# Moving the third exp reading from GpSimd to VectorE in a fused attention and FFN kernel

## The chip, the cores and the metric

The kernel runs on one core of a Trainium2 chip. The metric is the device time of one execution in microseconds (us), as the median of several runs. A core has five engines that run side by side and meet by semaphores: TensorE (PE; its weight loads are listed as PEld), VectorE (DVE), ScalarE (ACT), GpSimd (POOL) and SyncE (SP, which issues the DMAs). Matmul results lie in PSUM, eight banks of 128 x 512 f32; everything else lies in SBUF.

## The reference

```python
x = A_x                                  # (1, 2048, 640) bf16
xn = layernorm(x)
# A: 32 query heads of width 20, one shared key and value head
q = (xn @ wq) as (32 heads, 2048, 20);  k = xn @ wk;  v = xn @ wv      # k, v: (2048, 20)
p = softmax(q k^T * 20**-0.5)            # per head 2048 x 2048
a = (p @ v, heads side by side) @ wo
# B: FFN
b = silu(xn @ w1) @ w2                   # 640 -> 1728 -> 640
out = x + a + b
```

## The kernel before

**Tiling.** The 2048 queries are cut into 4 chunks of 512, so a head and a chunk make a unit, 128 units in all. Units go in groups of three (43 groups, the last with two). A group runs over 16 key tiles of 128 keys: 688 steps. In a step TensorE makes up to three score blocks (128 keys x 512 queries, L769), one per PSUM bank, in banks 0 to 2 and 3 to 5 in turn; the exp of each block is taken; and the exps are multiplied with the values (L857) into four 32-row strips of bank 6, where a group's sums pile up. Bank 7 serves all other matmuls: the projections, the FFN (L1084 for its first half, L1146 for its second) and the output projection (L1151).

**Exps by two engines.** ScalarE takes the exp of two or three blocks with one instruction (L787: 1024 or 1536 elements per partition). If `want_dve` says so, the step's third block goes to VectorE instead. There the scores come scaled so that an integer holds the bits of a bf16 number: one instruction (`p1`, L801) clamps a block and turns it into 16-bit integers Z, which read as bf16 are a coarse exp. To make it finer, the same bits are read three times: Z itself, Z + 43 and Z + 86, each with its own weighting of the values, and the three products are summed by TensorE. Z and the first addition's result (Y, index 0) enter at the step's own accumulation; the third reading (Y, index 1) enters as a "third" (`th` in `flush_z`), hosted by a step that has room for one more matmul, or by a separate accumulation `PT` for up to three of them.

**Who makes the readings.** Z + 43 is made by VectorE for up to three blocks at once (`flush_z`, L869, up to 1536 elements), when `ZB` blocks have gathered, after `ZWAIT` steps, or at a group's end. Z + 86 is made by GpSimd for each block at once, as `yp` (L807): it adds 86 * 65537 to pairs of 16-bit numbers read as one 32-bit integer. The constant lies in the tile `c86`, filled in the prologue.

**The order.** A planner in Python (`Sched`) builds the order of each engine before the kernel is emitted: it simulates the engines with estimated durations (`t_dve_4x`, `t_act` and so on) and picks for each engine the ready operation of lowest priority number; on VectorE p1 has 1.0, the evacuations of projections and the FFN 0.8, a group's evacuation of bank 6 (L972) 1.1, the readings 4.0. For TensorE `step` picks between score matmuls (first whenever their banks are free), accumulations and other jobs; accumulations are preferred when more than `NBLK - PV_PRESS` of the 31 blocks of the exp ring are in use. An operation with `lock` set is planned not to start while a locked one of the other engine (VectorE, GpSimd) runs: the readings and GpSimd's normalisations (L939 to L958) have it, `yp` has not (`Y_LOCK`). `Y_SLOW` adds 0.1 us to each planned reading. The chip runs each engine's list in the planned order, with waits on semaphores in place of the planned times.

What decides how many blocks VectorE gets:

```python
def want_dve(self, t):
    if t < DVE_FROM or t % KT >= KT - NOD or t >= self.T - DVE_LAST:
        return False
    sc = self.sc
    back = sc.t["dve"] - sc.t["pe"]
    for op in sc.pend["dve"]:
        back += op.dur
    back += len(self.zblocks) * 0.6
    return back < DVE_TH
```

Of the kernel before, what the change touches and what calls it, by code (L numbers as in the profile page):

```python
# [10 lines left out]
I32 = mybir.dt.int32  # L11
AF = mybir.ActivationFunctionType
ALU = mybir.AluOpType

P = 128
# [6 lines left out]
QW = 512  # L22
# [19 lines left out]
PH = ((0, 1.0), (43, 0.8046875), (86, 0.625))  # L42
# [3 lines left out]
NBLK = 31  # L46
NZ = 4
ZB = 3
Y_POOL = True
Y_TIME = 0.72  # L50
Y_LOCK = False
Y_SLOW = 0.1
H_FIRST = 4
NEARLY = 2
LASTPV = 16
# [1 line left out]
ZWAIT = 6  # L57
SWITCH = 0.105
S_LEAD = 0.56
PV_PRESS = 12  # L60
DVE_TH = 2.8
U_PRIO = 1.1
X_PRIO = 0.8
PACE = (0.9, 0.9, 0.9, 0.9)
# [251 lines left out]
def t_dve_4x(n):  # L316
    return n / 3840.0 + 0.065
# [37 lines left out]
class Builder:  # L355
# [13 lines left out]
    def sb(self, shape, dt):  # L369
        self.nsb += 1  # L370
        return self.stack.enter_context(self.nc.sbuf_tensor(f"sbt{self.nsb}", shape, dt))

    def alloc(self):
        sb = self.sb
        self.ps = self.stack.enter_context(self.nc.psum_tensor("psall", [P, 8 * BANK], F32))
        self.xnT = sb([P, DC, S], BF16)
        self.w1 = sb([P, DC, F], BF16)
        self.w2 = sb([P, FC, D], BF16)
        self.wq = sb([P, DC, D], BF16)
        self.qd = sb([P, 2, QW], BF16)  # L380
        self.wo = sb([P, DC, D], BF16)
        self.kT = sb([P, 2, S], BF16)
        self.v = sb([P, 5, KT, SLOT], BF16)
        self.qT = sb([P, HT, 2, QW], BF16)
        self.E = sb([P, NBLK * QW], BF16)
        self.Z = sb([P, NZ, ZB * QW], I16)
        self.Y = sb([P, NZ, 2, ZB * QW], I16)
        self.U = sb([P, 2, QW], BF16)
        self.kv_st = self.U[:, 1, 0:2 * DC * DH].rearrange("p (a c d) -> p a c d", a=2, c=DC)
        self.stk = sb([P, 64], BF16)  # L390
        self.UT = sb([P, 2, 4, P], BF16)
        self.W = sb([P, 4, 3, DH + 1], F32)
        self.hT = sb([P, FC, QW], BF16)
        self.o = sb([P, 4, D], BF16)
        self.oT = sb([P, DC, QW], BF16)
        self.wqp = self.oT[:, :, :].rearrange("p c e -> p (c e)")[:, 0:DC * 2 * P].rearrange("p (c e) -> p c e", c=DC)
        self.tb = sb([P, 2, QW], BF16)
        self.xres = sb([P, 4, D], BF16)
        self.yx = self.w1[:, :, :].rearrange("p a b -> p (a b)")[:, 0:8 * D].bitcast(F32).rearrange(
            "p (i e) -> p i e", i=4)  # L400
        self.ost = sb([P, 3, D], BF16)
        self.wk = self.ost[:, 2, :].rearrange("p (c e) -> p c e", c=DC)
        self.idf = self.w2[:, 4, 0:2 * P].bitcast(F32)
        self.idb = sb([P, P], BF16)
        self.st6 = sb([P, NT, 2, 6], F32)
        self.mv = sb([P, NT, 2], F32)
        self.rstd = sb([P, NT], F32)
        self.nb = sb([P, NT], F32)
        self.ex2 = sb([P, NT], F32)
        self.junk = self.E[:, (NBLK - 2) * QW:(NBLK - 2) * QW + D]  # L410
        self.tmp = sb([P, 4, NT], F32)
        self.rL = sb([P, 2, 4, 3], F32)
        self.offq = sb([P, 1], F32)
        self.offk = sb([P, 1], F32)
        self.eps = sb([P, 1], F32)
        self.c86 = sb([P, 1], I32)
        self.zero = sb([P, 512], BF16)
        self.XS = 11
        hflat = self.hT[:, :, :].rearrange("p a b -> p (a b)")
        oflat = self.o[:, :, :].rearrange("p b c -> p (b c)")  # L420
        self.okeys = [("o", h) for h in range(H)]

        def xslot(n):
            if n < self.XS:
                return hflat[:, n * D:(n + 1) * D]
            if n < NT - 1:
                return self.xres[:, n - self.XS, :]
            return oflat[:, 3 * D:4 * D]

        def xkeys(n):  # L430
            if n < self.XS:
                return [("hT_x", n)]
            if n < NT - 1:
                return [("xres", n - self.XS, 0), ("xres", n - self.XS, 1)]
            return [("x15",)] + self.okeys
        self.xslot = xslot
        self.xkeys = xkeys
# [312 lines left out]
    def do_S(self, t, now):  # L750
        sc = self.sc
        g, kt = divmod(t, KT)
# [40 lines left out]
        if dv:  # L793
            self.dve_steps += 1
            self.group_dve[g] += 1
            self.last_dve_kt[g] = kt
            zs, zp = self.zset, len(self.zblocks)
            bb = par3 + nh - 1

            def p1(v):  # L800
                return v.tensor_scalar(self.Z[:, zs, zp * QW:(zp + 1) * QW], self.bk(bb), 0.0, ZMAX,  # L801
                                       ALU.max, ALU.min)
            sc.new("dve", t_dve_ps(QW), p1, [("B", bb)], [("Z", zs, zp)], prio=1.0, name=f"p1_{t}")
            self.y_on_pool = Y_POOL
            if self.y_on_pool:
                c86 = bass.AP(self.c86, self.c86[:, :].offset, [list(self.c86[:, :].ap[0]), [0, QW // 2]])
                sc.new("pool", Y_TIME, lambda v: v.tensor_tensor(  # L807
                    self.Y[:, zs, 1, zp * QW:(zp + 1) * QW].bitcast(I32),
                    self.Z[:, zs, zp * QW:(zp + 1) * QW].bitcast(I32), c86, ALU.add),
                    [("Z", zs, zp), ("c86",)], [("Y", zs, 1, zp)], prio=4.0, name="yp").lock = Y_LOCK  # L810
        first = kt == 0
        last = kt == KT - 1

# [46 lines left out]
    def flush_z(self):  # L860
        sc = self.sc
        zs = self.zset
        n = len(self.zblocks)
        self.zset = (self.zset + 1) % NZ
        zk = [("Z", zs, i) for i in range(n)]
        Z = self.Z[:, zs, 0:n * QW]
        w = n * QW
        for k in range(1 if self.y_on_pool else 2):
            sc.new("dve", Y_SLOW + t_dve_4x(w), lambda v, k=k: v.tensor_scalar(  # L869
                self.Y[:, zs, k, 0:n * QW], Z, float(PH[k + 1][0]), None, ALU.add), zk,  # L870
                [("Y", zs, k, i) for i in range(n)], prio=4.0 + 0.1 * k, name=f"y{k}").lock = True
        ts = []
        for i, (t, pv) in enumerate(self.zblocks):
            ks = [("Z", zs, i), ("Y", zs, 0, i)]
            pv.deps |= sc.deps_of(ks, ())
            for k in ks:
                sc.readers[k].append(pv)
            x = self.Y[:, zs, 1, i * QW:(i + 1) * QW].bitcast(BF16)
            kt = t % KT

            def th(pe, q, x=x, kt=kt):
                if q >= 2:
                    return self.pv_mm(pe, q, 2, kt, x, False, False)
                self.pv_mm(pe, 0, 3, kt, x, False, False)
                return self.pv_mm(pe, 1, 4, kt, x, False, False)
            ts.append((th, ("Y", zs, 1, i), kt))
        first = self.zblocks[0][1]
        end = self.pv_wait[-1][0].kt == KT - 1
        tail = self.pv_wait.pop() if end else None
        seen = False  # L890
        for op, _ in self.pv_wait:
            seen = seen or op is first
            if seen and self.can_host(op) and ts:
                self.host(op, ts.pop())
        if end and self.can_host(tail[0]) and len(self.thirds + ts) % 3 == 1:
            self.host(tail[0], ts.pop() if ts else self.thirds.pop())
        self.thirds += ts
        while len(self.thirds) >= 3 or (end and self.thirds):
            part = self.thirds[:3]
            self.thirds = self.thirds[3:]  # L900

            def fn(pe, part=part):
                ins = None
                for q, x in zip((2, 3, 0), part):
                    ins = x[0](pe, q)
                return ins
            op = sc.new("pe", 0.3, fn, [x[1] for x in part], [], name="PT", mode="PV", queue=False)
            op.mm = len(part) + len(part) // 3
            op.kt = max(x[2] for x in part)
            op.na = 0  # L910
            op.after = None
            self.pv_wait.append((op, False))
        if tail is not None:
            self.pv_wait.append(tail)
        self.zblocks = []
# [368 lines left out]
    def prologue(self):  # L1284
# [49 lines left out]
        def pool(d, fn, r, w, prio=0.0):  # L1334
            return np_("pool", d, fn, r, w, prio=prio, name="pool")
# [4 lines left out]
        pool(0.2, lambda g: g.tensor_copy(self.idb[:, :], self.idf[:, :]), [("idf",)], [("idb",)])  # L1340
        pool(0.3, lambda g: g.memset(self.zero[:, :], 0.0), [], [("zero",)])
        pool(0.1, lambda g: g.memset(self.eps[:, :], EPS), [], [("eps",)])
        pool(0.1, lambda g: g.memset(self.c86[:, :], PH[2][0] * 65537), [], [("c86",)])
        pool(0.7, lambda g: g.memset(self.wk[:, :, :], 0.0), [], [("wk",), ("ost", 2, 0), ("ost", 2, 1)])
        wqd = self.wqp[:, :, :].rearrange("p c (h j) -> p c h j", j=SLOT)
        wqs = self.wq[:, :, 0:160].rearrange("p c (h d) -> p c h d", d=DH)
# [302 lines left out]
```

## Time and profile before

| | |
|---|---|
| median of 3 runs | 739.14 us (739.08 to 740.04) |
| profiled execution | 740.04 us, its span 738.2 us |
| granted TensorE clock | 0.995 |
| PE busy | 707.6 us, 96% |
| DVE busy | 665.5 us, 90% |
| ACT busy | 691.0 us, 94% |
| POOL busy | 538.4 us, 73% |
| `p1` L801 | 646 instructions |
| first addition L869 | 230 instructions |
| `yp` L807 | 646 instructions |

A row of a group reads: line, engine, operation, tiles out<-in, shapes out<-in, count | busy us of the group, mean ns of one | idle us of the engine just before them, and what ended most of that. A row of a stretch reads: window, its length, then for each engine busy us and instructions, then the granted clock, the DMA share and GB/s. A row of the waits reads: engine, tile and line that waited, what it waited for, total us, times, longest. A row of the timeline reads: start, us until the last of the merged instructions ends, engine and line, operation, count. A busy time holds the tail of an instruction that the next one may already overlap.

### The profile page before, as it was taken

To read this page: it belongs to the slowest core of one execution; us is meant where nothing else is said; L and a number is where in the kernel's file an instruction comes from. 1 tells how busy PE (TensorE), PEld (TensorE's weight loads), DVE (VectorE), ACT (ScalarE), POOL (GpSimd) and SP (SyncE) were. 2 spreads that over 40 slices of the span, in tenths; PEclk is the share of its full clock that TensorE was granted. 3 is DMA by queue.
4 is the path that set the end of the run, shared out by engine and by line. 5 is a ranking of instruction groups with operands and counts; after the bars stand their busy time and mean duration, and the time that the engine had idled before them with its cause. 6 is when DMAs were issued, how large, how long until landed. Compare 5 with 4: busy or idle time off the path is not lost.

```text
span 738.2 us, 18883 instructions
## 1 busy us (share of the span) xinstructions
PE 707.6 (96%) x6798; PEld 229.7 (31%) x6852; DVE 665.5 (90%) x1206; ACT 691.0 (94%) x780; POOL 538.4 (73%) x929
## 2 busy tenths in 40 slices
PE   9788999999999999999999999999999999999998
PEld 4422222233333223223333222222233332322235
DVE  7786998999999999989999999999999999989973
ACT  6886999999999999999999999999999999999940
POOL 5467777787787877777878877787788877777750
PEclk9999999999999999999999999999999999999999
DMA  6494010000003021100001101110002000200101
GB/s 191 80 338 108 20 25 17 21 17 16 9 16 44 17 58 40 32 10 9 9 8 27 33 16 40 54 32 16 8 9 44 10 8 16 80 9 8 31 16 36
DMA packets 58466, 29.14 MB, mean 39 GB/s; under 512 B 44390, under 2 KB 57734, under 8 KB 58374
## 3 DMA queue, kind: packets, MB, share of 16 engines
q1 hardware_dynamic: 56918, 27.71, 14.7%
q8 instruction: 56, 0.92, 0.5%
q10 hardware_dynamic: 1456, 0.22, 0.2%
q14 instruction: 36, 0.29, 0.1%
HBM read 11.36 MB, written 2.62 MB: 19 GB/s over the span
## 4 chain that ended last, share of the span: by engine, by line
PE 62%; ACT 17%; DVE 6%; issue 5%; POOL 1%; DMA 1%; DVEq 0%; ACTq 0%; POOLq 0%
PE psall L857 21%; PE psall L769 20%; ACT sbt L787 15%; PE psall L1146 9%; PE psall L1084 6%; DVE sbt L801 3%; PE psall L1151 2%; PE psall L1050 2%; ACT sbt L1092 1%; DVE sbt L869 1%; DMA sbt<-sbt 1%; DVE sbt L972 1%; PE psall L693 1%; POOL sbt L807 0%; DVE sbt L1057 0%
## 5 line engine op out<-in xcount | busy, mean ns | idle before, releaser
L787 ACT ACTIVATE sbt<-psall 128x1024 bf16<-128x1024 f32 (+2 forms) x688 | 657.8, 1091 | 16.8 <-PE psall L769 15.9
L807 POOL TENSOR_TENSOR sbt<-sbt 128x256 int32<-128x256 int32 x646 | 447.2, 698 | 149.3 <-DVE sbt L801 122.7
L801 DVE TENSOR_SCALAR sbt<-psall 128x512 int16<-128x512 f32 x646 | 432.5, 683 | 34.4 <-PE psall L769 26.4
L769 PE MATMUL psall<-sbt 32*128 32x512 bf16 x2048 | 269.1, 385 | 9.7 <-ACT sbt L787 4.7
L857 PE MATMUL psall<-sbt 128*32 128x512 bf16 x3524 | 270.2, 385 | 4.2 <-DVE sbt L869 2.0
L769 PEld LDWEIGHTS psall<-sbt 32*128 32x128 bf16 x2048 | 68.7, 91 | 252.8 <-issue 105.1
L869 DVE TENSOR_SCALAR sbt<-sbt 128x1536 int16<-128x1536 int16 (+2 forms) x230 | 134.8, 587 | 2.8
L857 PEld LDWEIGHTS psall<-sbt 128*32 128x32 bf16 x3524 | 67.8, 94 | 115.0 <-issue 75.4
L1146 PE MATMUL psall<-sbt 128*128 128x320 bf16 x448 | 86.2, 302 | 0.0
L1084 PE MATMUL psall<-sbt 128*128 128x512 bf16 (+1 forms) x242 | 75.7, 385 | 5.1 <-issue 3.7
L1146 PEld LDWEIGHTS psall<-sbt 128*128 128x128 bf16 x448 | 35.1, 97 | 43.4 <-issue 33.8
L1097 DVE SCALAR_TENSOR_TENSOR sbt<-sbt,psall 128x512 bf16<-128x512 bf16 (+1 forms) x56 | 38.1, 680 | 4.2 <-ACT sbt L1092 3.5
L1092 ACT ACTIVATE sbt<-psall 128x512 bf16<-128x512 f32 (+1 forms) x56 | 37.7, 674 | 0.0
L1084 PEld LDWEIGHTS psall<-sbt 128*128 128x128 bf16 (+1 forms) x280 | 18.8, 98 | 39.9 <-issue 29.6
L972 DVE CAST sbt<-psall 128x512 bf16<-128x512 f32 x43 | 29.3, 681 | 2.0 <-PE psall L857 1.9
L1151 PE MATMUL psall<-sbt 128*128 128x320 bf16 x144 | 28.7, 303 | 0.4 <-DVE sbt L1181 0.4
L1050 PE MATMUL psall<-sbt 128*128 128x512 bf16 (+1 forms) x81 | 26.6, 385 | 2.4 <-issue 1.4
L958 POOL TENSOR_TENSOR sbt<-sbt 128x240 bf16<-128x240 f32 (+2 forms) x44 | 25.7, 583 | 0.9 <-DMA sbt<-sbt 0.5
L944 POOL TENSOR_TENSOR sbt<-sbt 128x44 f32<-128x44 f32 x84 | 25.0, 298 | 1.0
L706 PE MATMUL psall<-sbt 128*128 128x512 bf16 (+2 forms) x67 | 17.5, 407 | 4.8 <-DVE sbt L1565 3.3
L942 POOL CAST sbt<-sbt 128x168 f32<-128x168 bf16 x42 | 14.2, 337 | 9.7 <-DMA sbt<-sbt 9.1
L1178 ACT ACTIVATE sbt<-psall 128x320 bf16<-128x320 f32 x4 | 1.5, 437 | 20.7 <-PE psall L1151 20.7
(94 smaller groups left out, 219.8 us busy)
## 6 DMA issues: line engine op xcount, KB each, us to landing
sbt<-in_A_x_dram SPq DMA_DIRECT2D x32, 160.0 KB, 3.6
out_dram<-sbt SPq DMA_DIRECT2D x15, 160.0 KB, 1.9
sbt<-in_B_w_dram SPq DMA_DIRECT2D x5, 432.0 KB, 7.4
sbt<-sbt SPq DMA_DIRECT2D x105, 20.0 KB
sbt<-in_B_w_dram SPq DMA_DIRECT2D x13, 160.0 KB, 5.8
sbt<-sbt SPq DMA_TRANSPOSE x68, 2.4
sbt<-sbt SPq DMA_DIRECT2D x1, 1024.0 KB, 7.3
sbt<-in_A_wo_dram SPq DMA_DIRECT2D x5, 160.0 KB, 6.8
```

The lines of the kernel that those rows point to most:

```text
L769: ins = pe.matmul(self.bk(par3 + j), self.kT[r:r + SLOT, kk, kt * P:(kt + 1) * P], self.qT[r:r + SLOT, h // 4, (x // H) % 2, :], start=Tru ...
L787: return a.activation(self.E[:, b0 * QW:(b0 + na) * QW], self.ps[:, par3 * BANK:(par3 + na) * BANK], AF.Exp, scale=ACT_SCALE)
L801: return v.tensor_scalar(self.Z[:, zs, zp * QW:(zp + 1) * QW], self.bk(bb), 0.0, ZMAX, ALU.max, ALU.min)
L807: sc.new("pool", Y_TIME, lambda v: v.tensor_tensor(self.Y[:, zs, 1, zp * QW:(zp + 1) * QW].bitcast(I32), self.Z[:, zs, zp * QW:(zp + 1) * ...
L857: return pe.matmul(self.bk(UBANK, 0, QW, q * SLOT, (q + 1) * SLOT), self.v[:, w, kt, :], x, start=start, stop=stop, tile_position=(0, q * ...
L869: sc.new("dve", Y_SLOW + t_dve_4x(w), lambda v, k=k: v.tensor_scalar(self.Y[:, zs, k, 0:n * QW], Z, float(PH[k + 1][0]), None, ALU.add), z ...
L1050: return pe.matmul(self.bk(b, 0, QW, 0, rows), self.wq[:, k, lo:hi], self.xnT[:, k, c * QW:(c + 1) * QW], start=(k == 0), stop=(k == DC - 1))
L1084: return pe.matmul(self.bk(b, 0, QW, 0, rows), self.w1[:, k, fk * P:fk * P + rows], self.xnT[:, k, c * QW:(c + 1) * QW], start=(k == 0), s ...
L1092: sc.new("act", t_act(QW), lambda a: a.activation(t, src, AF.Tanh, scale=0.5), [("B", b)], [("tb", tp)], prio=X_PRIO, name=f"th{c}_{fk}")
L1097: sc.new("dve", t_dve_ps(QW), lambda v: v.scalar_tensor_tensor(out=self.hT[0:rows, fk, :], in0=t, scalar=1.0, in1=src, op0=ALU.add, op1=AL ...
L1146: return pe.matmul(self.bk(b, 0, 320), self.hT[0:rows, fk, i * P:(i + 1) * P], self.w2[0:rows, fk, e0:e0 + 320], start=(m == 0), stop=(m = ...
L1151: return pe.matmul(self.bk(b, 0, 320), self.oT[:, k, i * P:(i + 1) * P], self.wo[:, k, e0:e0 + 320], start=(m == 0 and src != "ps"), stop= ...
```

## The change

`yp` and its constant `c86` are taken out. `flush_z` makes both additions on VectorE, Z + 43 and Z + 86, as two instructions one behind the other over the same gathered blocks. The planner's extra 0.1 us on a reading goes, `PV_PRESS` becomes 8 and `DVE_TH` 3.2. TensorE's use of the readings is the same.

```diff
-Y_POOL = True
-Y_TIME = 0.72
-Y_LOCK = False
-Y_SLOW = 0.1
...
-PV_PRESS = 12
-DVE_TH = 2.8
+PV_PRESS = 8
+DVE_TH = 3.2
...
-        self.c86 = sb([P, 1], I32)
...
             sc.new("dve", t_dve_ps(QW), p1, [("B", bb)], [("Z", zs, zp)], prio=1.0, name=f"p1_{t}")
-            self.y_on_pool = Y_POOL
-            if self.y_on_pool:
-                c86 = bass.AP(self.c86, self.c86[:, :].offset, [list(self.c86[:, :].ap[0]), [0, QW // 2]])
-                sc.new("pool", Y_TIME, lambda v: v.tensor_tensor(
-                    self.Y[:, zs, 1, zp * QW:(zp + 1) * QW].bitcast(I32),
-                    self.Z[:, zs, zp * QW:(zp + 1) * QW].bitcast(I32), c86, ALU.add),
-                    [("Z", zs, zp), ("c86",)], [("Y", zs, 1, zp)], prio=4.0, name="yp").lock = Y_LOCK
...
-        for k in range(1 if self.y_on_pool else 2):
-            sc.new("dve", Y_SLOW + t_dve_4x(w), lambda v, k=k: v.tensor_scalar(
+        for k in range(2):
+            sc.new("dve", t_dve_4x(w), lambda v, k=k: v.tensor_scalar(
                 self.Y[:, zs, k, 0:n * QW], Z, float(PH[k + 1][0]), None, ALU.add), zk,
                 [("Y", zs, k, i) for i in range(n)], prio=4.0 + 0.1 * k, name=f"y{k}").lock = True
...
-        pool(0.1, lambda g: g.memset(self.c86[:, :], PH[2][0] * 65537), [], [("c86",)])
```

## The prediction

> **What bounds the kernel now.** I read the table of busy time by stretch first, because the kernel has a ramp, a long uniform middle and a tail.
>
> ```profile
> core 0: us, PE busy (x) PEld busy (x) DVE busy (x) ACT busy (x) POOL busy (x), PEclk, DMA share, GB/s
> ...
> 60.00:100.00 40.00, 35.96 (x323) 10.32 (x327) 31.77 (x56) 34.45 (x40) 30.72 (x53) 0.96 0.10 20
> 100.00:150.00 50.00, 47.99 (x458) 13.92 (x462) 46.00 (x78) 50.00 (x58) 36.20 (x61) 1.00 0.08 20
> ...
> 300.00:350.00 50.00, 47.60 (x451) 14.63 (x449) 45.81 (x77) 50.00 (x59) 37.96 (x63) 1.00 0.04 10
> ...
> 450.00:500.00 50.00, 48.73 (x472) 14.34 (x475) 48.42 (x84) 50.00 (x56) 38.41 (x64) 1.00 0.17 41
> ```
>
> From 100 to 700 us ScalarE (ACT) is idle for at most 0.3 us in any 50: it sets the pace. TensorE looks almost as busy, but matmul ends are modelled. VectorE (DVE) is close behind, and GpSimd (POOL) has 9 to 14 us free in 50. DMA is idle. Next, the groups by shape say what these engines do:
>
> ```profile
> L787 ACT ACTIVATE sbt<-psall 128x1024 bf16<-128x1024 f32 x632 | 597.4, 1077 | 10.9 <-PE psall L769 10.4
> L807 POOL TENSOR_TENSOR sbt<-sbt 128x256 int32<-128x256 int32 x646 | 447.2, 698 | 149.3 <-DVE sbt L801 122.7 <-PE psall L769 9.8 <-PE psall L857 2.5
> L801 DVE TENSOR_SCALAR sbt<-psall 128x512 int16<-128x512 f32 x646 | 432.5, 683 | 34.4 <-PE psall L769 26.4 <-POOL sbt L944 1.0 <-POOL sbt L939 0.4
> ...
> L869 DVE TENSOR_SCALAR sbt<-sbt 128x1536 int16<-128x1536 int16 x198 | 119.1, 602 | 2.7
> ...
> L787 ACT ACTIVATE sbt<-psall 128x1536 bf16<-128x1536 f32 x41 | 60.8, 1489 | 2.6 <-PE psall L769 2.5
> ```
>
> There are 688 steps of up to three score blocks. A step whose third block goes to VectorE costs ScalarE a 1024-wide exp, otherwise a 1536-wide one: 1.489 - 1.077 = 0.412 us more. So **each block that VectorE gives back costs the bound engine 0.41 us**. VectorE has 646 blocks already; 41 steps are 1536 wide.
>
> The timeline says what an instruction takes from its engine, since its mean duration holds a tail that the next one overlaps:
>
> ```profile
> 301.11 1.27 DVE L801 TENSOR_SCALAR sbt<-psall 128x512 int16<-128x512 f32 x2
> 302.42 0.56 DVE L869 TENSOR_SCALAR sbt<-sbt 128x1536 int16<-128x1536 int16 x1
> 302.90 1.28 DVE L801 TENSOR_SCALAR sbt<-psall 128x512 int16<-128x512 f32 x2
> ```
>
> Two blocks end 1.27 us after the first starts, so the second starts 1.27 - 0.68 = 0.59 later: 0.60 us each (its median from start to start). The 1536-wide reading takes 302.90 - 302.42 = 0.48 (median 0.476).
>
> **The change part by part.** *What moves.* For each VectorE block GpSimd made the third reading (Y, index 1) at L807. These 646 instructions go; `flush_z` makes it as a second instruction behind the first, for up to three blocks at once. The bits are the same, so TensorE's work per block stays.
>
> *VectorE's load now*, in the 600 us from 100 to 700, by starts in the trace: 578 blocks x 0.60 = 347. Of the 204 readings (182 of 1536 elements, 12 of 1024, 10 of 512) the wide ones lie beside GpSimd and last 0.602 on average, against 0.555 for those that don't start inside a GpSimd instruction: 0.475 + 0.047 = 0.52 each, all 204 together 103. FFN products 50 x 0.60 = 30, accumulator evacuations 38 x 0.60 = 23, queries 16 x 0.60 = 10, output sums 49 x 0.40 = 20, reciprocals 38 x 0.14 = 5. Sum 538, 90% of 600. (The busy row's 94% holds the tails.)
>
> *VectorE's load after, if no block moves*: the readings become clean pairs, 182 x 0.95 + 12 x 0.68 + 10 x 0.4 = 185 in place of 103. Sum 620: 103% of the time there is. It can't fit, so the planner, which offers VectorE a block only while its backlog is under `DVE_TH`, hands blocks to ScalarE, whose work is the time.
>
> *How many.* With x blocks given back, each frees 0.60 + 2 x 0.475/3 = 0.92 us of VectorE and lengthens the stage by 0.41: 620 - 0.92x = u(600 + 0.41x), u being the share of VectorE that the planner can fill. At u = 1, x = 15 and the stage is 6.2 us longer. At 0.98, which is what ScalarE fills as the bound (578 x 0.904 + 31 x 1.331 + 50 x 0.477 + 0.75 = 589 of 600), x = 24, 10 us. At 0.90, today's fill, x = 62, 25.4 us. I take 0.96, x = 33.5, **13.7 us**: nearer to ScalarE's row, because a queue that always has a ready reading in it has fewer gaps than today's. Its fullest stretch (450 to 500) is already 97% by the busy row, but its instructions come in bursts behind the FFN jobs, so not 0.98.
>
> *What y pairs do to score banks.* A block behind a reading waits; a block releases the score bank that the matmul two steps on needs. Now:
>
> ```profile
> PEld psall L769 <- ACT sbt L787: 63.9, 166, 0.7
> ...
> PEld psall L769 <- DVE sbt L801: 42.7, 108, 0.6
> ...
> PEld psall L769 <- DVE sbt L869: 9.2, 23, 0.5
> ...
> PEld psall L857 <- POOL sbt L807: 5.8, 21, 1.3
> ```
>
> Readings were the last thing 23 times. A pair keeps a block 0.475 longer: 23 x 0.4 = 9 us more if all of it reached ScalarE; zero if its exp in hand (0.9 us) covers it. I take **1.5**, nearer to zero, because today's 52 us of waits for VectorE leave ScalarE only 16.8 us idle in all. Queued behind such a block on VectorE are the FFN products (L1097), which hold bank 7, and the evacuation of the accumulator (L972).
>
> *The ramp* (40 to 100 us): 51 blocks, 17 readings, 17 x 0.43 = 7 us more in some 11 idle us of VectorE. 0 to 3, I take **0.5**: a block may be given back. *The tail*: the last third reading came 0.61 us after its block from an idle GpSimd, now 0.475 after its first reading, so 0.3 later; 0 to 1, I take **0.2**.
>
> *Priced at nothing.* GpSimd's freed 447 us: only 5.8 + 0.8 us of matmul waits and 4.0 us of reciprocal waits hung on it, and what waited for it waits for the second reading next; a gain of up to 6 stays in the range. TensorE's 34 fewer third readings free some 22 quartets of matmuls, 22 x 0.23 = 5 us, beside a ScalarE that is never idle. The `c86` memset lies in the ramp, where GpSimd is 60% busy. `PV_PRESS` 8 for 12 lets more exp blocks wait before the accumulation is preferred, so TensorE's order changes: -2 to +2, taken as 0, since score matmuls go first in either. `DVE_TH` and `Y_SLOW` act through u.
>
> *Sum*: 13.7 + 1.5 + 0.5 + 0.2 = 15.9. The profiled execution took 740.04 (span 738.2 and 1.8 around it), 0.9 over the median of three runs, 739.14. So 755.9 against the profiled one and **755** as a median.
>
> **A rule against the row.** In the trace 100 of the 198 wide readings start inside a GpSimd instruction; they last 0.643, the others 0.555. A GpSimd addition that starts inside a reading lasts 0.887, an undisturbed one 0.612. So the offload costs VectorE 9 us in all, and saves it some 90.
>
> The Trainium skill (Perfetto Trace Analysis, Optimizing Scalar/DVE Operations) warns that VectorE and GpSimd share an SBUF port, so that moving work between them may not help. Taken at its word, undoing the move would cost nothing and the time would stay at 739. By the rows it is GpSimd that pays most of the sharing, and the sum stays at 755.
>
> **The rivals.** *Faster*: the second readings fit, no block is given back, and TensorE's waits for GpSimd (5.8 us) go: about 733. It needs VectorE at 0.98 of 600 (588) with 538 - 103 + 93 = 528 (the first readings clean) plus the second ones, so at most 60 us for 204, 0.29 each. The row says 0.475, and the second instruction has nothing to overlap but the tail already taken off. Only if a pair ran much closer than a reading and a block do. *Nearly free*: VectorE fills to 0.98 or more, nothing else: 739 + 6.2 to 739 + 10, 745 to 750. For it: with both readings on one engine no lock breaks the queue. *Stalls*: pairs hold up blocks and thereby score matmuls, so VectorE stays at 0.90 and ScalarE gets gaps: 25.4 + 5 = 30, 764 to 773. For it: 31 of these 610 steps are already 1536 wide although VectorE is 90% full, so bursts count. *No effect*: GpSimd's readings held something that I don't see, worth the same 16: 739.
>
> **How the numbers follow.** The forecast (u of 0.98 with a gap of 1 us, 739 + 10 + 1, to u of 0.93, where x = 47.6 costs 19.5, with gaps of 5: 750 to 764) gets 0.60, nearly free 0.19, stalls 0.13, faster 0.05, no effect 0.03. A measurement can tell a change of about 0.2% (1.5 us) from none. Slower: 0.60 + 0.19 + 0.13 = 0.92; same 0.03; faster 0.05. The range from 745 to 766 takes in the forecast and nearly free, leaving out most of the stalls and both cases at or under 739.
>
> **What would show it.** Right: no int32 group on GpSimd, whose busy time falls to about 90; some 430 readings in the reading group, with a mean of 0.55 to 0.57; about 610 blocks at L801's successor instead of 646 and about 77 exps of 1536 elements instead of 41; ScalarE still without idle time from 100 to 700 and about 14 us busier; VectorE's busy row at 97% or more. Wrong: as many blocks as before; ScalarE idle for over 10 us in the middle (then stalls on score banks are the price, not blocks); or VectorE under 94%.

## The result and the profile after

The kernel after takes 745.80 us (median of four runs, 744.75 to 746.59) against 739.59 for the kernel before in the same comparison: ratio 1.0079, 95% interval 1.0056 to 1.0103. It is slower by 6.2 us, where the prediction had 15.9. The profiled execution took 745.05 us with a span of 743.2, 5.0 more than the 738.2 of before.

The same stretches of the table of busy time, after:

```profile
core 0: us, PE busy (x) PEld busy (x) DVE busy (x) ACT busy (x) POOL busy (x), PEclk, DMA share, GB/s
...
60.00:100.00 40.00, 35.62 (x308) 9.96 (x312) 36.36 (x66) 34.86 (x39) 10.58 (x20) 0.91 0.07 18
100.00:150.00 50.00, 47.54 (x448) 13.91 (x453) 48.63 (x90) 50.00 (x57) 6.79 (x15) 1.00 0.07 18
...
300.00:350.00 50.00, 48.08 (x446) 14.25 (x451) 49.12 (x91) 50.00 (x59) 6.31 (x15) 1.00 0.05 10
...
450.00:500.00 50.00, 47.93 (x458) 14.42 (x463) 49.08 (x93) 50.00 (x56) 8.17 (x19) 1.00 0.10 28
```

ScalarE still has no idle time in the middle. VectorE went from 564 to 586 busy us of the 600 from 100 to 700. The groups by shape (L782, L796 and L857 are the lines that were L787, L801 and L869):

```profile
L782 ACT ACTIVATE sbt<-psall 128x1024 bf16<-128x1024 f32 x597 | 571.2, 1084 | 13.7 <-PE psall L764 13.2
L796 DVE TENSOR_SCALAR sbt<-psall 128x512 int16<-128x512 f32 x605 | 403.1, 682 | 11.2 <-PE psall L764 8.0
...
L857 DVE TENSOR_SCALAR sbt<-sbt 128x1536 int16<-128x1536 int16 x348 | 189.2, 557 | 1.2
L782 ACT ACTIVATE sbt<-psall 128x1536 bf16<-128x1536 f32 x79 | 118.3, 1504 | 2.8 <-PE psall L764 2.7
```

41 blocks went back to ScalarE (605 on VectorE, from 646), 79 exps are 1536 wide (from 41), and the wide readings, now in pairs, last 0.557 instead of 0.602. All this is close to the prediction. ScalarE's busy time rose from 691.0 to 708.3, by 17.3 us. The last exp ends 19.2 us later, as the timelines of ScalarE show, first before, then after (start, length; the second line merges two exps):

```profile
712.08 1.02 ACT L787 ACTIVATE sbt<-psall 128x1024 bf16<-128x1024 f32 x1 [0.68 <-PE psall L769]
```

```profile
730.77 1.51 ACT L782 ACTIVATE sbt<-psall 128x512 bf16<-128x512 f32 x2 [0.36 <-PE psall L764]
```

So the exps end at 713.1 before and at 732.3 after. The kernel ends 25.1 us after that before, and 10.9 after. **The exps became longer by more than predicted, and the tail behind them became 14.2 us shorter**: 19.2 - 14.2 = 5.0, the difference of the spans. What the tail held, in TensorE's timeline of before:

```profile
714.51 1.33 PE L1146 MATMUL psall<-sbt 128*128 128x320 bf16 x7
715.68 0.28 PE L984 MATMUL psall<-sbt 128*128 128x64 bf16 x4
715.80 1.49 PE L1146 MATMUL psall<-sbt 128*128 128x320 bf16 x9
717.22 0.40 PE L1124 MATMUL psall<-sbt 128*128 128x128 bf16 x4
717.46 10.61 PE L1146 MATMUL psall<-sbt 128*128 128x320 bf16 x70
728.00 2.35 PE L1151 MATMUL psall<-sbt 128*128 128x320 bf16 x16
```

L1146 is the second half of the last chunk's FFN. Of its 112 matmuls 86 start after the last exp, at 10.61/70 = 0.15 us each 13 us of TensorE, while ScalarE has nothing to do and VectorE is busy for 7 of 19 us. In after none of the 112 does; the last starts at 715.7, among the exps. The stretches of L1134 alone, which is this line in after, show none behind 720:

```profile
core 0: us, PE busy (x), PEclk, DMA share, GB/s
...
700.00:720.00 20.00, 7.78 (x43) 1.00 0.16 28
720.00:760.00 40.00, 0.00 (x0) 1.00 0.08 24
```

The row of the waits that shows the tail at a glance is ScalarE's wait for the first of its four closing evacuations, before and after:

```profile
ACT sbt L1178 <- PE psall L1151: 20.7, 1, 20.7
```

```profile
ACT sbt L1166 <- PE psall L1139: 6.5, 1, 6.5
```

### The profile page after: what moved, and what is told of

It reads as the page before. It is cut to its first block, busy times and chain, and to the rows that moved or that the text cites. A ratio compares the mean times of both kernels' runs of the same rounds, so it can differ in the third digit from the quotient of the medians.

```text
span 743.2 us, 17728 instructions
## 1 busy us (share of the span) xinstructions
PE 708.9 (95%) x6725; PEld 229.5 (31%) x6783; DVE 703.5 (95%) x1369; ACT 708.3 (95%) x780; POOL 111.3 (15%) x282
## 3 DMA queue, kind: packets, MB, share of 16 engines
q1 hardware_dynamic: 56918, 27.71, 14.4%
## 4 chain that ended last, share of the span: by engine, by line
PE 62%; ACT 23%; DVE 8%; issue 5%; DMA 1%; POOL 1%; ACTq 0%; DVEq 0%; POOLq 0%
ACT sbt L782 20%; PE psall L764 20%; PE psall L845 19%; PE psall L1134 8%; PE psall L1072 6%; DVE sbt L796 3%; ACT sbt L1080 2%; PE psall L1139 2%; PE psall L1038 2%; PE psall L701 2%; DVE sbt L857 2%; PE psall L688 1%; DMA sbt<-sbt 1%; PE psall L1519 1%; DVE sbt L960 0%
## 5 line engine op out<-in xcount | busy, mean ns | idle before, releaser
L782 ACT ACTIVATE sbt<-psall 128x1024 bf16<-128x1024 f32 (+2 forms) x688 | 675.7, 1124 | 18.6 <-PE psall L764 17.9
L796 DVE TENSOR_SCALAR sbt<-psall 128x512 int16<-128x512 f32 x605 | 403.1, 682 | 11.2 <-PE psall L764 8.0
L845 PE MATMUL psall<-sbt 128*32 128x512 bf16 x3427 | 260.4, 386 | 4.3 <-DVE sbt L857 2.9
L857 DVE TENSOR_SCALAR sbt<-sbt 128x1536 int16<-128x1536 int16 (+2 forms) x434 | 221.7, 530 | 1.3
L845 PEld LDWEIGHTS psall<-sbt 128*32 128x32 bf16 x3427 | 66.0, 94 | 112.8 <-issue 73.6
L930 POOL CAST sbt<-sbt 128x168 f32<-128x168 bf16 x42 | 16.1, 384 | 516.8 <-DMA sbt<-sbt 516.8
L1134 PE MATMUL psall<-sbt 128*128 128x320 bf16 x448 | 87.1, 303 | 0.3 <-DVE sbt L1151 0.3
L1072 PE MATMUL psall<-sbt 128*128 128x512 bf16 (+1 forms) x241 | 75.3, 386 | 5.2 <-issue 3.0
L1134 PEld LDWEIGHTS psall<-sbt 128*128 128x128 bf16 x448 | 33.7, 97 | 44.3 <-issue 35.3
L946 POOL TENSOR_TENSOR sbt<-sbt 128x240 bf16<-128x240 f32 (+2 forms) x44 | 28.2, 641 | 72.8 <-DVE sbt L937 59.4
L1038 PE MATMUL psall<-sbt 128*128 128x512 bf16 (+1 forms) x78 | 24.4, 383 | 2.6 <-issue 1.3
L688 PE MATMUL psall<-sbt 128*32 128x512 bf16 (+7 forms) x80 | 23.5, 353 | 0.0
L927 POOL TENSOR_TENSOR sbt<-sbt 128x84 f32<-128x84 bf16 x42 | 16.7, 397 | 0.0
```

The lines of the kernel that those rows point to most:

```text
L782: return a.activation(self.E[:, b0 * QW:(b0 + na) * QW], self.ps[:, par3 * BANK:(par3 + na) * BANK], AF.Exp, scale=ACT_SCALE)
L845: return pe.matmul(self.bk(UBANK, 0, QW, q * SLOT, (q + 1) * SLOT), self.v[:, w, kt, :], x, start=start, stop=stop, tile_position=(0, q * ...
L857: sc.new("dve", t_dve_4x(w), lambda v, k=k: v.tensor_scalar(self.Y[:, zs, k, 0:n * QW], Z, float(PH[k + 1][0]), None, ALU.add), zk, [("Y", ...
L1038: return pe.matmul(self.bk(b, 0, QW, 0, rows), self.wq[:, k, lo:hi], self.xnT[:, k, c * QW:(c + 1) * QW], start=(k == 0), stop=(k == DC - 1))
L1072: return pe.matmul(self.bk(b, 0, QW, 0, rows), self.w1[:, k, fk * P:fk * P + rows], self.xnT[:, k, c * QW:(c + 1) * QW], start=(k == 0), s ...
L1134: return pe.matmul(self.bk(b, 0, 320), self.hT[0:rows, fk, i * P:(i + 1) * P], self.w2[0:rows, fk, e0:e0 + 320], start=(m == 0), stop=(m = ...
```

## The experiments

*The question.* Two theories fit the two traces, before and after. In the ScalarE theory the 41 blocks lengthen the exps, and the FFN matmuls move into the longer exps at no cost. In the TensorE theory TensorE's total work sets the end, and the exps end later because FFN matmuls now stand between the score matmuls. A third possibility is that the constant `PV_PRESS`, and not the longer exps, moved the FFN forward. Ratios are to the kernel before, with 95% intervals.

### The FFN of the last chunk cut, in both kernels

```diff
-        tot = (FC if ffn else 0) + len(ks)
+        tot = ((FC if c < QC - 1 else 1) if ffn else 0) + len(ks)
...
-            for fk in range(FC):
+            for fk in range(FC if c < QC - 1 else 1):
```

> The kernel before, but each FFN sum of the last chunk takes 1 of its 14 matmuls (13 x 8 = 104 matmuls of L1146 left out, 104 x 0.133 = 13.8 us of TensorE). In the trace of before 110 or so of the 112 ran alone after the exps had nearly ended. Both theories: 739.6 - 13.8 = 726, 724 to 729.

> The kernel after with the same 104 matmuls left out; there they run beside the exps. ScalarE theory (the exps end 19 us later because 41 more blocks went to ScalarE, and the FFN matmuls moved into that time for nothing): the exps end as late as before, 742 to 746, so 16 to 20 above the run of before with the same cut. TensorE theory (TensorE's total work sets the end, and the exps end later because the FFN matmuls now stand between the score matmuls): 745.8 - 13.8 = 732, 730 to 734, so 6 above that run.

Before with the cut: 727.23 us (0.9829, 0.9813 to 0.9845). After with the cut: 743.17 us (1.0041, 1.0030 to 1.0053). The last exps, in the timelines of ScalarE, before with the cut and after with it:

```profile
713.06 1.02 ACT L787 ACTIVATE sbt<-psall 128x1024 bf16<-128x1024 f32 x1 [0.78 <-PE psall L1151]
```

```profile
729.95 1.02 ACT L782 ACTIVATE sbt<-psall 128x1024 bf16<-128x1024 f32 x1 [3.09 <-PE psall L764]
```

Taking the matmuls out of before saves 12.5 us (739.71 - 727.23), all of it behind the exps, which end at 714.1 instead of 713.1. That fits the 86 matmuls which the trace has there (the expectation's 110 was too many). Taking them out of after saves 2.6 (from 745.80 in the first comparison), and there the exps still end at 731.0. So the 104 matmuls hardly delay the exps of after: they lie beside them for nearly nothing. The ScalarE theory's numbers held, the TensorE theory's 732 fell. With this FFN out of both tails the two kernels are 743.17 - 727.23 = 15.9 us apart. That is the prediction's number, though not by the same terms (see below).

### The FFN of the last chunk kept back in after

```diff
             gate = lambda: (c, i, e) in self.y_done
+        elif ffn and c == QC - 1:
+            gate = lambda: self.s_next >= self.T
```

> The kernel after, with the last chunk's FFN sums kept back until the last score matmul has been ordered, so that they run behind the exps as in before. ScalarE theory: the exps don't end earlier, the 13.8 us come on top: 756 to 760, which is what the prediction had (755). TensorE theory: the same work in another order, 744 to 748.

761.18 us (1.0286, 1.0267 to 1.0305), 15.4 above after. ScalarE's wait in the tail:

```profile
ACT sbt L1166 <- PE psall L1139: 24.5, 1, 24.5
```

110 of the 112 matmuls start behind the last exp, at 0.15 us 16.5 us; the exps end at 730.6, hardly earlier than the 732.3 of after. The order of the same work is worth 15 us, which the TensorE theory doesn't allow. The time is 1.2 us over the expected range, which priced a matmul at 0.133 us where before's tail shows 0.15.

### Blocks given back, with GpSimd still reading

```diff
+        if t % 16 == 7:
+            return False
         if t < DVE_FROM or t % KT >= KT - NOD or t >= self.T - DVE_LAST:
```

> The kernel before (GpSimd makes the third readings), with VectorE refused a block at every key tile 7: 613 blocks on VectorE in place of 646, so 33 back on ScalarE, 33 x 0.41 = 13.6 us. ScalarE theory: the exps end some 14 us later and 9 to 13 us of FFN matmuls move in beside them: 740 to 745. The prediction's rule (what ScalarE gets is what the time grows by): 753. TensorE theory: 33 third readings fewer, some 5 us of matmuls less, 734 to 738.

745.40 us (1.0069, 1.0045 to 1.0092), as slow as the change, with GpSimd's readings in place and VectorE at 533 of 600 us. ScalarE's busy time is 705.8, 14.7 more; the exps end at 727.5, 14.4 later; 14 FFN matmuls instead of 86 are left behind them, and the wait in the tail is half as long:

```profile
ACT sbt L1180 <- PE psall L1153: 10.0, 1, 10.0
```

So it takes neither the pairs of readings nor a full VectorE to get this result, only blocks given back. The time is 0.4 us over the expected range, and the 5.7 us that it grew by are far from the 13.6 that the blocks cost ScalarE.

A block given back also takes its readings' matmuls from TensorE, which is a second source of room. L857 (L845 in after) is the line that multiplies the exps with the values:

```profile
L857 PE MATMUL psall<-sbt 128*32 128x512 bf16 x3524 | 270.2, 385 | 4.2 <-DVE sbt L869 2.0 <-POOL sbt L807 0.8 <-DVE sbt L972 0.5
```

```profile
L845 PE MATMUL psall<-sbt 128*32 128x512 bf16 x3427 | 260.4, 386 | 4.3 <-DVE sbt L857 2.9 <-DVE sbt L960 1.0 <-issue 0.3
```

At the prediction's 0.23 us for four, the 97 matmuls fewer are an estimated 5.6 us. The 13 us of FFN don't fit into that alone, but no run separates it from the longer exps.

### PV_PRESS, in both directions

> The kernel after with PV_PRESS at 12 as before. 609 blocks on VectorE, 28 matmuls of the output sums behind the last exp instead of 8. If the longer exp stage makes the room for the FFN matmuls (ScalarE theory): the FFN is still nearly all beside the exps, 20 x 0.133 = 2.7 us come behind, 746 to 751. If it was this constant that moved the FFN forward: most of the 13.8 us come back, 755 to 760.

```diff
-PV_PRESS = 8
+PV_PRESS = 12
```

750.62 us (1.0145, 1.0128 to 1.0163). The exps end at 734.2 and four FFN matmuls are left behind them. The constant didn't move the FFN: undoing it costs 4.8 us, but doesn't bring the tail back.

> The kernel before with PV_PRESS at 8 as after: 648 blocks on VectorE, GpSimd reads, 50 matmuls of the output sums behind the last exp instead of 110. If TensorE had idle room beside before's exps and only the order was at fault (constant theory): 60 x 0.133 = 8 us gained, 731 to 734. If there is no room, since TensorE and ScalarE are both full there (ScalarE theory with a full TensorE): what moves in delays the score matmuls by as much or more, and the exps end later: 739 to 750.

```diff
-PV_PRESS = 12
+PV_PRESS = 8
```

746.92 us (1.0097, 1.0081 to 1.0113). Here 26 FFN matmuls are left behind the exps instead of 86, and yet the end is 7.4 us later, because the exps end at 728.3, 15.2 later, with ScalarE's work nearly unchanged (692.6 against 691.0). Its plan also has a poorer ramp: from 40 to 100 us ScalarE is busy for 45.3 us against 51.1. So a part of the 15 us, some 6, need not be the FFN's doing. From 100 to 700 us ScalarE's waits for scores rose from 0.8 to 4.3 us, so another part is TensorE's. Before's FFN can't be had earlier for free in this way; how much of the price is TensorE's fullness is not settled by this run.

### The mirror: more blocks to VectorE

```diff
-Y_TIME = 0.72
+Y_TIME = 0.66
...
-Y_SLOW = 0.1
+Y_SLOW = 0.03
...
-DVE_TH = 2.8
+DVE_TH = 2.9
```

> The mirror of the change: the kernel before with cheaper planned readings and a higher threshold (Y_SLOW 0.03, DVE_TH 2.9, Y_TIME 0.66), so that VectorE gets 664 blocks, 18 more, and ScalarE loses 18 x 0.41 = 7.4 us. The prediction's rule: 7.4 us faster, 732. If the FFN behind the exps is what the time is traded against: the exps end 7 us earlier or more, the tail grows by as much, the end stays, 737 to 742.

743.65 us (1.0052, 1.0037 to 1.0066). ScalarE's busy time fell by 6.4 us to 684.6, and the exps ended at 702.2, 10.9 earlier. The kernel took 4.1 us longer all the same (743.65 against 739.56). From 702 on:

```profile
core 0: us, PE busy (x) PEld busy (x) DVE busy (x) ACT busy (x) POOL busy (x), PEclk, DMA share, GB/s
...
702.00:712.00 10.00, 9.74 (x73) 3.81 (x67) 7.02 (x15) 3.75 (x7) 0.90 (x2) 1.00 0.01 2
712.00:737.00 25.00, 23.48 (x161) 14.78 (x159) 7.50 (x15) 1.14 (x3) 0.00 (x0) 1.00 0.00 1
```

TensorE is busy for 33 of these 35 us, now with some of the FFN's first half too, and ScalarE for 5. What ScalarE gains, the tail takes back, and more: the time is 2 us over the expected range.

> The kernel before with Y_SLOW at 0.05, which is what the trace shows a reading to lose beside GpSimd (0.602 against 0.555), instead of 0.1: 655 blocks on VectorE, 9 more. The prediction's rule: 9 x 0.41 = 3.7 us faster, 736. The trade between exps and tail: no more than 2 us either way, 738 to 742.

```diff
-Y_SLOW = 0.1
+Y_SLOW = 0.05
```

739.94 us (1.0002, 0.9993 to 1.0011): no difference. The exps end at 710.2, 2.9 earlier than before; the wait in the tail is 23.1 instead of 20.7.

### DVE_TH alone, undone

```diff
-DVE_TH = 3.2
+DVE_TH = 2.8
```

> The kernel after with DVE_TH at 2.8 as before: 588 blocks on VectorE, 17 more to ScalarE, 17 x 0.41 = 7.0 us. In after nothing of the FFN is left behind the exps to move in, so a block given back must now cost its full price or more: 753 or more (ScalarE theory). If the slope seen between before and after (6.2 us for 41 blocks, 0.15 us a block) held on: 748 to 749.

760.54 us (1.0281, 1.0264 to 1.0298). The direction is the ScalarE theory's, but the size proves little: ScalarE's work rose by only 6.8 us (715.1), while in this plan's ramp, from 40 to 100 us, it is busy for 39.5 us against 52.6 in after. Those 13 us are a poorer plan, not blocks, so the price of one block with no FFN left in the tail can't be read from this run.

## Why the prediction was right or wrong

**Which engine, right.** VectorE could not take the second reading, the planner handed blocks to ScalarE, and ScalarE stayed without idle time in the middle. The fill came out at u = 0.953 (VectorE's instructions by their start-to-start times are 572 of 600 us in after), taken as 0.96; 41 blocks against 33.5; ScalarE +17.3 us against 13.7. The prediction's rule of 0.41 us a block gives 41 x 0.41 = 16.9.

**The stalls, too dear.** 1.5 us were put on pairs holding up score matmuls. Score matmuls waited for a reading 30 times, 11.9 us, instead of 23 times, 9.2 us:

```profile
PEld psall L764 <- DVE sbt L857: 11.9, 30, 0.5
```

ScalarE's waits for scores between 100 and 700 us fell from 0.8 to 0.2. The pair as a whole doesn't hold up a block, since blocks and FFN products have the better priority and go between its two readings, as VectorE's timeline of after shows:

```profile
301.41 0.55 DVE L857 TENSOR_SCALAR sbt<-sbt 128x1536 int16<-128x1536 int16 x1
301.87 0.68 DVE L1085 SCALAR_TENSOR_TENSOR sbt<-sbt,psall 128x512 bf16<-128x512 bf16 x1
302.47 0.55 DVE L857 TENSOR_SCALAR sbt<-sbt 128x1536 int16<-128x1536 int16 x1
302.98 0.69 DVE L796 TENSOR_SCALAR sbt<-psall 128x512 int16<-128x512 f32 x1
```

**The step that failed: the tail, taken at +0.2 us.** The prediction looked only at the latency of the last third reading there, and its sum let every microsecond of the exps reach the end. The tail was -14.2, and that term is off by 14.4 us. The rest of the sum, what moves the end of the exps, was 15.7 and came out at 19.2, 3.5 more: 15.9 + 3.5 - 14.4 = 5.0. The row that pointed to the tail, ScalarE's wait of 20.7 us, stood in the waits of before, beside a stretch in which TensorE was busy throughout. It was work put off for want of time beside the exps, and the longer exps gave it that time, perhaps with a little room from the matmuls that went away. With the work put back behind the exps, after is at 761, 6 us above the forecast of 755, and some 4 of them are because 110 matmuls lie there and not 86 (24 x 0.15). So the mechanism of the main term was right, and the tail's term had the wrong size and sign.

That the two kernels without this work differ by 15.9 us, the sum to the decimal, is partly luck. The sum had 33.5 blocks and 1.5 us of stalls; these two kernels differ by 39 blocks (643 and 604), which at 0.41 us are 16.0, and by 15.8 us of ScalarE's busy time (692.6 and 708.4).

The same step explains why "TensorE's 34 fewer third readings ... beside a ScalarE that is never idle" was the wrong reason to price TensorE at nothing: ScalarE was idle behind the exps, and TensorE was the engine that ended last.

**The constants, mis-sized.** `PV_PRESS` was taken as 0, within 2 us either way, because score matmuls go first in either setting. Undoing it in after costs 4.8 us, and setting it in before costs 7.4. `DVE_TH` was left to act through u alone; undoing it costs 14.7 us, with 13 us less ScalarE work done in the ramp. So the 6.2 us are the price of VectorE's second reading together with the constants that came along with it; what it costs without them, no run shows.

**Smaller points.** GpSimd's busy time is 111 us, not about 90. The 90 was 538 less the 447 of the third readings, but instructions overlap in GpSimd's records: by their own durations its other work adds up to 105 us before and 115 after. Some 8 of these 10 us are the normalisations, which became slower (last section). 434 readings came, 430 were expected. VectorE's row is at 97.7%, as expected. Of the rivals, "nearly free" had a time of 745 to 750, where the measured one lies, but for another reason: VectorE did not fill to 0.98, and 41 blocks were given back, not 15 to 24. The time alone would have confirmed the wrong case.

**The rule.** The Trainium skill (Perfetto Trace Analysis, Optimizing Scalar/DVE Operations) warned that work moved between VectorE and GpSimd may gain nothing because of the shared port. Here the kernel whose third readings are on GpSimd is the faster one by 6.2 us, each kernel with its own constants, and by 15.9 with the FFN's tail cut.

## What to carry to other kernels

An engine that is never idle in the middle sets the time only if nothing was put off behind it: before adding a cost to the sum, read what runs after its last instruction, and subtract from the cost what can move in beside it. The reverse holds too, as the mirror shows: relieving the busiest engine buys nothing once another engine has a tail of its own to finish. A measured time inside one rival's range says little until the counts of that rival's mechanism (here blocks given back, and matmuls behind the last exp) are read from the trace.

## What the runs showed of the hardware

VectorE's readings and GpSimd's instructions wait for each other. With the readings in pairs on VectorE, GpSimd's own work, the same 42 normalisations, became slower although GpSimd had less to do. One of its groups before, and the same one (L939 became L927) after:

```profile
L939 POOL TENSOR_TENSOR sbt<-sbt 128x84 f32<-128x84 bf16 x42 | 14.5, 345 | 0.0
```

```profile
L927 POOL TENSOR_TENSOR sbt<-sbt 128x84 f32<-128x84 bf16 x42 | 16.7, 397 | 0.0
```

The mean hides two populations. In after 35 of the 42 meet no reading and last 0.344 us as before. Of the 7 that overlap one, five start inside a reading: they last 0.65 us, and each ends 0.20 us after that reading. A sixth meets two readings and lasts 1.01, to 0.21 us after the second; the seventh meets only the last 0.03 us and lasts 0.34.

An addition of before (L807) that starts inside a reading is held back in the same way, as this pair of its timeline shows: it ends 0.47 us after the reading, and lasts 0.99 instead of 0.612.

```profile
308.47 0.56 DVE L869 TENSOR_SCALAR sbt<-sbt 128x1536 int16<-128x1536 int16 x1
...
308.51 0.99 POOL L807 TENSOR_TENSOR sbt<-sbt 128x256 int32<-128x256 int32 x1 [0.27 <-DVE sbt L801]
```

It holds the other way round too. By the trace's starts 102 of the 198 wide readings of before start inside a GpSimd instruction (the prediction counted 100). The 64 of them that have more than 0.14 us of it before them all end 0.41 to 0.42 us after it, whether 0.15 or 0.59 us of it were left; the other 38 last 0.55 on average, like undisturbed ones. So the mean of 0.643 in the prediction is not one of slower readings: most wait until GpSimd is done, and the rest lose nothing.

The planner keeps GpSimd's normalisations and the readings from starting inside one another, but the chip follows its order and not its times.
